# Attention scores and their gradients as 128-column products on four 32-row strips, in a kernel that computes a gated block and its gradients

## The chip, the cores and the metric

The kernel runs on one core of one Trainium2 chip, as one program. The metric is device time in microseconds (us), from the timed runs of the program; lower is better. The engines are named as in the profile: PE is TensorE (matrix products and transposes), ACT is ScalarE, DVE is VectorE, POOL is GpSimd, SP is the engine that issues most DMAs.

## What is computed

A forward pass of two branches mixed by a gate, and the gradients of all its inputs but one (everything in bf16, x is 2048 x 512):

```python
def _A_ref(x, wqkv, wo):                      # attention, 32 heads of 16, window 256
    q, k, v = split_heads(x @ wqkv)
    scores = einsum("bhqd,bhkd->bhqk", q, k) * (Dh ** -0.5)
    mask = (iq - ik >= 0) & (iq - ik < 256)
    p = softmax(where(mask, scores, -1e9))
    return merge_heads(einsum("bhqk,bhkd->bhqd", p, v)) @ wo

def _B_ref(x, W_gate, W_up, W_down):          # gated MLP, inner width 1376
    gate, up = x @ W_gate, x @ W_up
    return ((gate * (gate > 0)) * up) @ W_down

g = sigmoid((x * gate_w).sum(-1))
out = g * _A_ref(x, wqkv, wo) + (1 - g) * _B_ref(x, W_gate, W_up, W_down)
# outputs: out, and its gradients with respect to x, wqkv, wo, W_gate, W_up, W_down, gate_w
```

## The kernel before

It has three stages. The first (lines 189 to 456) computes the MLP branch, its weight gradients, and the inputs of attention's backward pass. The last (lines 920 to 997) sums the output and the gradient of x for 16 row tiles of 128. The change lies almost wholly in the stage between them, attention forward and backward (lines 458 to 916).

Attention works on four chunks of eight heads (`c`), and in each on 16 query blocks of 128 (`j`). A query block meets its own key block and the two before it. `project_parts` (lines 119 to 187) makes, for one chunk and four query blocks (a group), the tiles Q, dO, K and V with (head, dimension) on the 128 partitions, so that a strip of 32 partitions holds two heads of 16. K and V are kept in two copies, each with every second head's rows set to zero (`K0`, `K1`, lines 153 to 160).

A unit (lines 627 to 641) is one query block, one key block and one half of the chunk's heads, four heads: 90 units a chunk, 360 in all. `front` (line 643) computes its scores in one product of 128 rows and 512 columns (`ST`, line 649). The moving operand is a tile `z` in which the four strips of Q stand block-diagonally with zeros around them; `spread` (line 468) fills it with four DMAs a group. ACT takes the exponential (line 655), POOL masks the diagonal and the far key block with a 512-column `affine_select` (lines 657 and 660), and `front_dp` (line 663) makes the gradient with respect to the probabilities the same way (`dPT`, line 669). `gradp` (line 671) multiplies both on DVE. `rowsum` (line 676) makes 8 small products a unit into one PSUM bank, `BA`, from which POOL works out each query block's terms (`small_ops`, line 711). `flip` (line 694) transposes a unit's two results: 159 units by a DMA transpose that SP issues (line 697), 201 by eight transposes on TensorE into a PSUM bank of the tag `TR` (line 706) and one copy of 1024 columns, on ACT and DVE in turn. `cd_piece` (line 480) makes the products for the gradients of K and V from the flipped tiles. `grad_parts` (line 557) makes the weight gradients of the last chunk.

The order is written out by hand. The loop at line 821 goes through the units one by one. Each step issues the scores of unit n, DVE's product of unit n-1, the DMA flip of unit n-2, row sums and TensorE's flip of unit n-3, then `front_dp` of unit n, then CD pieces, and then, as a running credit allows (lines 872 to 897), one piece of the next group's projection or of the last chunk's weight gradients. PSUM has eight banks: four of the tag `M` (scores, their gradients, projections, weight gradients), two `TR`, one `CD`, one `BA`.

Of the kernel before, what the change touches and what calls it, by code (L numbers as in the profile page):

```python
# [22 lines left out]
def kernel(  # L23
# [82 lines left out]
    ZB = 2  # L106
    wq = ctx.enter_context(tc.tile_pool(name="wq", bufs=1))
    zt = [wq.tile([P, 2, TPG, NP, P], BF, tag=f"z{i}", name=f"z{i}") for i in range(ZB)]
# [4 lines left out]
    if True:  # L113
# [5 lines left out]
        def project_parts(c, tg):  # L119
# [3 lines left out]

            def mm(nm, which, eng):
                ps, tag, bufs, _ = pools["now"]
                pp = ps.tile([P, TGW], F32, tag=tag, bufs=bufs, name="pp")
                for cd in range(DC):
                    if which < 3:
                        nc.tensor.matmul(pp[:], lhsT=w_p[c][:, cd, which * P:(which + 1) * P], rhs=x_T[tg][:, cd, :],  # L129
                                         start=(cd == 0), stop=(cd == DC - 1))  # L130
                    else:
                        nc.tensor.matmul(pp[:], lhsT=w_p[c][:, cd, 3 * P:4 * P], rhs=da_T[tg][:, cd, :],
                                         start=(cd == 0), stop=(cd == DC - 1))
                if nm in ("Q", "dO"):
                    if nm == "Q":
                        t4["z"] = pjA.tile([P, 2, TGW], BF, tag="zT", name="zT")
# [8 lines left out]
                if nm in ("Q", "dO"):  # L145
                    if c == 0 and tg == 0:
                        w = ("Q", "dO").index(nm)
                        for k in range(NP):
                            rows = slice(32 * k, 32 * k + 32)
                            evac(zt[0][rows, w, :, k, :], dst[rows, :].rearrange("p (k q) -> p k q", k=TPG),  # L150
                                 (("dve", "act")[w] if k % 2 else "dve"))
                else:
# [9 lines left out]
            def tr(a_nm, b_nm):  # L162
                ps, tag, bufs, trt = pools["now"]
                pt = ps.tile([P, 2, TPG, P], BF, tag=trt, bufs=2, name="ptp")
# [11 lines left out]
            def tr_kv():  # L176
# [9 lines left out]
            return [lambda: mm("Q", 0, "dve"), lambda: mm("dO", 3, "dve"), tr_rows, lambda: mm("K", 1, "act"),  # L186
                    lambda: mm("V", 2, "act"), tr_kv]

    with ExitStack() as p1, tc.manual_schedule():
# [20 lines left out]
        def load_go(tg):  # L210
            flat = zt[tg // 2][:].rearrange("p w k h q -> p (w k h q)")
            go_in[tg] = flat[:, (tg % 2) * TPG * D:(tg % 2 + 1) * TPG * D].rearrange("p (t d) -> p t d", t=TPG)
            nc.sync.dma_start(go_in[tg], rows_of(go_d, tg))
# [186 lines left out]
        pools["now"] = (ps1, "tr", 2, "tr")  # L400
# [3 lines left out]
        for n in range(N1 + 8):  # L404
# [38 lines left out]
            if t in (NT + 3, NT + 5):  # L443
                i = (t - NT - 3) // 2
                nc.gpsimd.memset(zt[i][:, 0, :, :, :], 0.0)
                nc.vector.memset(zt[i][:, 1, :, :, :], 0.0)
            if n == N1 - 2:
                first = project_parts(*groups[0])
            for _ in range({N1 + 1: 2, N1 + 2: 0}.get(n, 1)):
                if first:  # L450
                    first.pop(0)()
# [7 lines left out]
    if True:  # L459
# [7 lines left out]
        pools["now"] = (ps, "M", 4, "TR")  # L467
        def spread(gi, k):
            rows = slice(32 * k, 32 * k + 32)
            nc.sync.dma_start(zt[gi % ZB][rows, :, :, k, :],  # L470
                              proj[groups[gi]]["z"][rows, :, :].rearrange("p w (k q) -> p w k q", k=TPG))

# [7 lines left out]
        def cd_piece(c, kb, qb, half, last):  # L480
# [4 lines left out]
            p2 = P2[(c, qb, kb, half)]  # L485
            for hh in range(HH):
                h = 2 * hh + half
                nc.tensor.matmul(cd[0][:, h, :], lhsT=p2[:, 0, hh, :], rhs=rq[:, h, 0:2 * Dh],  # L488
                                 start=cd[1], stop=True, skip_group_check=True)
                cd[1] = False  # L490
                nc.tensor.matmul(cd[0][:, h, 0:Dh], lhsT=p2[:, 1, hh, :], rhs=rq[:, h, 2 * Dh:3 * Dh],  # L491
                                 start=False, stop=True, skip_group_check=True)
# [47 lines left out]
        def load_wo():  # L540
            t = pjA.tile([P, 2, TGW], BF, tag="zT", name="wo_z")
# [15 lines left out]
        def grad_parts(c, rest=None):  # L557
# [13 lines left out]
            hold = {}  # L571

# [7 lines left out]
            def piece(part, t0, first, last):  # L580
                if first:
                    tag, bufs = ("TR", 2) if part == DC and rest is not None else ("M", 4)
                    hold[part] = ps.tile([P, 3, P] if part < DC else [P, D], F32, tag=tag, bufs=bufs, name="wps")
                wps = hold[part]
                for t in range(t0, t0 + 4):
                    go_, no_ = first and t == t0, last and t == t0 + 3
                    if part < DC:
                        nc.tensor.matmul(wps[:], lhsT=x_r[:, t, part * P:(part + 1) * P], rhs=sts[c][:, t, 0:3, :],  # L588
                                         start=go_, stop=no_)
                    else:  # L590
                        nc.tensor.matmul(wps[:], lhsT=sts[c][:, t, 3, :], rhs=rows[t], start=go_, stop=no_)
                if not last:
                    return None
                if part < DC:
                    ws = (gwp if rest is None else S2["t6"]).tile([P, 3, P], BF, tag="ws", bufs=2 if rest is None else 5, name="ws")
                    evac(ws[:], wps[:], "act" if rest is None or part % 2 else "dve")
                    return store(part, ws)
                if t0 + 4 < NT:
                    hold["half"] = gwp.tile([P, D], F32, tag="half", bufs=1, name="half")
                    evac(hold["half"][:], wps[:], "act")  # L600
                    for k in range(4, 8):
                        load_da(k)
                    return None
                ws = (gwp if rest is None else S2["t6"]).tile([P, D], BF, tag="ws", bufs=2 if rest is None else 5, name="ws")
                if "half" in hold:
                    nc.vector.tensor_tensor(out=ws[:], in0=hold["half"][:], in1=wps[:], op=ALU.add)
                else:
                    evac(ws[:], wps[:], "act")
                return store(part, ws)

            if rest is None:
                parts = [(DC, 0, NT // 2)] + [(p, 0, NT) for p in range(DC)] + [(DC, NT // 2, NT)]
# [6 lines left out]
            for part, a, b in parts:  # L619
                for t0 in range(a, b, 4):  # L620
                    out.append((lambda part=part, t0=t0, f=(t0 == a), l=(t0 + 4 == b): piece(part, t0, f, l), t0 + 4 < b))
# [5 lines left out]
        units = []  # L627
        for c in range(DC):
            for j in range(NT):
                kbs = [k for k in (j - 1, j, j - 2) if k >= 0]  # L630
                for half in range(2):
                    order = kbs if half or len(kbs) < 3 else [kbs[0], kbs[2], kbs[1]]
                    for ki, kb in enumerate(order):
                        u = Unit()
                        u.c, u.j, u.kb, u.half = c, j, kb, half
                        u.first = ki == 0 and half == 0
                        u.last = ki == len(kbs) - 1 and half == 1
                        u.role = ("d", "m", "f")[j - kb]
                        u.dma = (u.role == "d" or (u.role == "m" and half == 0 and j % 2 == 1)) and (c < DC - 1 or j < NT - 2)
                        units.append(u)  # L640
        NU = len(units)

        def front(u):
            tg, jl = u.j // TPG, u.j % TPG
            z = zt[(u.c * NTG + tg) % ZB]
            KTt = proj[(u.c, u.kb // TPG)][f"K{u.half}"]
            ksl = slice((u.kb % TPG) * P, (u.kb % TPG + 1) * P)
            ST = ps.tile([P, HH, P], F32, tag="M", bufs=4, name="ST")
            nc.tensor.matmul(ST[:], lhsT=KTt[:, ksl], rhs=z[:, 0, jl, :, :], start=True, stop=True)  # L649
            if u.dma or u.role == "d":  # L650
                u.PP = wk.tile([P, 2, HH, P], BF, tag="PP", bufs=5, name="PP")
                u.Pu, u.Pd = u.PP[:, 0, :, :], u.PP[:, 1, :, :]
            else:
                u.Pu = wk.tile([P, HH, P], BF, tag="Pu", bufs=3, name="Pu")
            nc.scalar.activation(u.Pu[:], ST[:], ACT.Exp)  # L655
            if u.role == "d":
                nc.gpsimd.affine_select(out=u.Pu[:], in_=u.Pu[:], compare_op=ALU.is_ge, fill=0.0, base=0,  # L657
                                        pattern=[[0, HH], [1, P]], channel_multiplier=-1)
            elif u.role == "f":
                nc.gpsimd.affine_select(out=u.Pu[:], in_=u.Pu[:], compare_op=ALU.is_ge, fill=0.0, base=-1,  # L660
                                        pattern=[[0, HH], [-1, P]], channel_multiplier=1)

        def front_dp(u):
# [364 lines left out]
```

## Time and profile before

| | us |
|---|---|
| timed runs: median of 3 (lowest, highest) | 968.82 (966.36, 969.21) |
| the profiled execution: its time | 971.04 |
| its span, first to last instruction | 969.0 |
| attention stage in it, first score product to the first product of the last weight gradients | 517.9 |

The profile page gives each engine's busy time and a map of 40 slices of the span. The trace behind it answers for a window, a line of the kernel, or a tile. Matrix products are pipelined, so one product's duration in the trace is its latency; what it costs TensorE is the distance from its start to the next start. A group's row in the profile reads: line, engine, operation, output and inputs with their shapes, count, then busy time in us and the mean duration of one in ns, then idle time before it and what ended it.

### The profile page before, as it was taken

The page shows a single profiled execution, that of the slowest core. Times are in us where ns is not written, and L with a number is a line of the kernel's source. Part 1 is how long each engine was busy: PE and PEld are TensorE (multiplying, and loading weights), DVE is VectorE, ACT ScalarE, POOL GpSimd, SP SyncE. Part 2 cuts the span into 40 slices and gives each one's busy share as a digit, 9 for nine tenths or more (in the row PEclk, how much of TensorE's full clock was granted, in tenths as well). Part 3 has the DMA queues.
Part 4 walks back from the last instruction along what each step waited for, and adds up shares of the span by engine and source line. Part 5 has one row for each costly group of instructions (what it writes and reads, how often), then busy time and mean ns, then how long its engine had stood idle before and what let it go on. Part 6 is the DMA issues. An engine that isn't in the chain of part 4 may idle for free.

```text
span 969.0 us, 27638 instructions
## 1 busy us (share of the span) xinstructions
PE 938.9 (97%) x11281; PEld 598.3 (62%) x11281; DVE 501.5 (52%) x918; ACT 473.8 (49%) x811; POOL 488.4 (50%) x936
## 2 busy tenths in 40 slices
PE   7999999999999999999999999989999999999998
PEld 4556555656567777676776677756777754444443
DVE  4443323323377777666776667765667613223322
ACT  5422322222378777667776667766677720001001
POOL 2644345444177667666676556665657622121211
PEclk9999999999999999999999999998999999999999
DMA  9988899996667598985889857899999969866760
GB/s 291 185 201 206 218 218 210 220 196 174 143 114 122 100 160 155 154 146 100 145 126 189 138 103 139 127 162 175 160 141 229 185 184 260 194 171 165 183 155 28
DMA packets 447415, 161.64 MB, mean 167 GB/s; under 512 B 365784, under 2 KB 444984, under 8 KB 447288
## 3 DMA queue, kind: packets, MB, share of 16 engines
q1 hardware_dynamic: 424888, 136.80, 73.8%
q10 hardware_dynamic: 20592, 17.84, 6.1%
q0 software_dynamic: 1808, 5.24, 1.5%
q8 instruction: 88, 1.44, 0.7%
q14 instruction: 39, 0.32, 0.1%
HBM read 38.44 MB, written 38.41 MB: 79 GB/s over the span
## 4 chain that ended last, share of the span: by engine, by line
PE 82%; DMA 6%; POOL 4%; SPq 2%; DVE 2%; ACT 1%; issue 1%; ACTq 0%; POOLq 0%; DVEq 0%
PE pt L706 9%; PE dxps L970 8%; PE ST L649 7%; PE dPT L669 7%; PE wps L373 6%; PE wps L588 4%; PE dxps L991 4%; PE BA L683 4%; PE pp L129 4%; PE bps L941 4%; PE CD L488 4%; PE dhps L326 3%; PE ups L326 3%; PE dps L375 3%; PE gps L326 3%; PE CD L491 2%
## 5 line engine op out<-in xcount | busy, mean ns | idle before, releaser
L674 DVE TENSOR_TENSOR Pd<-Pu,dPT 128x512 bf16<-128x512 bf16 x201 | 136.6, 681 | 64.9 <-POOL Pu L660 53.5
L655 ACT ACTIVATE Pu<-ST 128x512 bf16<-128x512 f32 x201 | 121.6, 606 | 58.9 <-PE ST L649 57.3
L649 PE MATMUL ST<-z,K 128*128 128x512 bf16 x360 | 136.8, 380 | 4.0 <-DVE Pd L674 1.7
L669 PE MATMUL dPT<-z,V 128*128 128x512 bf16 x360 | 137.2, 381 | 1.3 <-DVE Pd L674 1.1
L674 DVE TENSOR_TENSOR PP<-PP,dPT 128x512 bf16<-128x512 bf16 x159 | 108.4, 682 | 41.0 <-POOL PP L657 38.1
L657 POOL TENSOR_SCALAR_AFFINE_SELECT PP<-PP 128x512 bf16<-128x512 bf16 x128 | 81.3, 635 | 79.5 <-ACT PP L655 78.8
L655 ACT ACTIVATE PP<-ST 128x512 bf16<-128x512 f32 x159 | 95.7, 602 | 51.7 <-PE ST L649 42.0
L340 POOL TENSOR_TENSOR hT<-rg,upm 128x512 bf16<-128x512 bf16 x44 | 52.2, 1186 | 123.9 <-DVE upm L338 98.4
L488 PE MATMUL CD<-rq,p 128*128 128x32 bf16 x1440 | 109.7, 177 | 0.8 <-ACT rows_st L494 0.5
L373 PE MATMUL wps<-dgu_r,x_r 128*128 128x256 bf16 x704 | 105.6, 272 | 4.9 <-DVE wst L74 4.9
L491 PEld LDWEIGHTS <-p 128*128 128x128 bf16 x1440 | 86.4, 96 | 35.9 <-issue 3.1
L72 ACT COPY p<-pt 128x1024 bf16<-128x1024 bf16 x103 | 105.1, 1020 | 5.2 <-PE pt L706 2.5
L491 PE MATMUL CD<-rq,p 128*128 128x16 bf16 x1440 | 106.7, 169 | 0.0
L488 PEld LDWEIGHTS <-p 128*128 128x128 bf16 x1440 | 99.0, 96 | 1.7 <-issue 1.5
L660 POOL TENSOR_SCALAR_AFFINE_SELECT Pu<-Pu 128x512 bf16<-128x512 bf16 x112 | 71.0, 634 | 41.8 <-ACT Pu L655 40.1
L373 PEld LDWEIGHTS <-x_r 128*128 128x128 bf16 x704 | 68.8, 98 | 36.7 <-issue 6.3
L948 ACT COPY a_sb<-aps 128x512 f32<-128x512 f32 x16 | 9.4, 585 | 145.8 <-issue 133.1
L706 PE MATMUL pt<-ident,Pd 128*128 128x128 bf16 x804 | 78.4, 220 | 0.0
L706 PE MATMUL pt<-ident,Pu 128*128 128x128 bf16 x804 | 77.7, 219 | 0.0
L74 DVE COPY p<-pt 128x1024 bf16<-128x1024 bf16 x102 | 69.5, 681 | 6.1 <-PE pt L706 5.4
L332 ACT ACTIVATE rg<-gps 128x512 bf16<-128x512 f32 x44 | 26.3, 598 | 91.0 <-PE gps L326 49.6
L683 PE MATMUL BA<-KV,Pu 128*128 128x33 bf16 x804 | 66.6, 178 | 4.1 <-ACT BAs L689 4.0
(158 smaller groups left out, 1998.7 us busy)
## 6 DMA issues: line engine op xcount, KB each, us to landing
dqkvo_d<-rows_st SPq DMA_DIRECT2D x7, 1024.0 KB, 5.7
dar<-da_d SPq DMA_DIRECT2D x28, 256.0 KB, 4.3
hT_d<-hT ACTq DMA_DIRECT2D x44, 128.0 KB, 2.4
dgT_d<-dgu ACTq DMA_DIRECT2D x44, 128.0 KB, 2.8
duT_d<-dgu ACTq DMA_DIRECT2D x44, 128.0 KB, 2.8
duT_g<-duT_d SPq DMA_DIRECT2D x8, 640.0 KB, 5.2
dgT_g<-dgT_d SPq DMA_DIRECT2D x7, 640.0 KB, 9.1
gt<-hT_d SPq DMA_DIRECT2D x7, 640.0 KB, 5.7
```

The lines of the kernel that those rows point to most:

```text
L72: nc.scalar.copy(out, in_)
L326: nc.tensor.matmul(out[:], lhsT=w(c), rhs=x(c), start=(c == 0), stop=(c == DC - 1))
L373: nc.tensor.matmul(acc["w"][:, c, :], lhsT=x_r[:, t, c * P:(c + 1) * P], rhs=k.dgu_r[:, :, i, :], start=(go_ and c % 2 == 0), stop=no_, sk ...
L488: nc.tensor.matmul(cd[0][:, h, :], lhsT=p2[:, 0, hh, :], rhs=rq[:, h, 0:2 * Dh], start=cd[1], stop=True, skip_group_check=True)
L491: nc.tensor.matmul(cd[0][:, h, 0:Dh], lhsT=p2[:, 1, hh, :], rhs=rq[:, h, 2 * Dh:3 * Dh], start=False, stop=True, skip_group_check=True)
L649: nc.tensor.matmul(ST[:], lhsT=KTt[:, ksl], rhs=z[:, 0, jl, :, :], start=True, stop=True)
L655: nc.scalar.activation(u.Pu[:], ST[:], ACT.Exp)
L657: nc.gpsimd.affine_select(out=u.Pu[:], in_=u.Pu[:], compare_op=ALU.is_ge, fill=0.0, base=0, pattern=[[0, HH], [1, P]], channel_multiplier=-1)
L669: nc.tensor.matmul(u.dPT[:], lhsT=VTt[:, ksl], rhs=z[:, 1, jl, :, :], start=True, stop=True)
L674: nc.vector.tensor_tensor(out=u.Pd[:], in0=u.Pu[:], in1=u.dPT[:], op=ALU.mult)
L683: nc.tensor.matmul(BA[:, h, 0:33], lhsT=u.Pu[:, hh, :], rhs=kv[:, u.kb % TPG, h, 1:34], start=(u.first and hh == 0), stop=True, skip_group ...
L706: nc.tensor.transpose(pt[:, a, hh, :], src[:, hh, :], ident[:])
```

## The change

The zero-padded tile `z` and its DMAs are gone. A unit is now one strip of 32 partitions (two heads, `g` from 0 to 3) and two key blocks; a turn works on two units. The loop goes through 46 turns a chunk, 184 in all, for six turns per pair of query blocks: `d` and `e` units pair the diagonal and the far block, `m` units the two middle blocks. In each turn TensorE makes the scores of this turn's two units and the gradients of the last turn's two as 16 products of 32 rows and 128 columns, issued in rotation over the four strips. Each unit has a PSUM bank of its own: two banks `S`, two `D`. Projections, weight gradients and TensorE's flips share the two banks `tr`.

```diff
+                its = ((d, (0, 1)), (m, (2, 3)), (m, (0, 1)), (d, (2, 3)), (e, (0, 1)), (e, (2, 3)))
...
+                        u.dma = g % 2 == 0 and u.nb == 2 and (c > 0 or j > 0) and (c < DC - 1 or j < NT - 2)
...
+        def score(u, nm, w, out):
+            rows = slice(32 * u.g, 32 * u.g + 32)
+
+            def one(i, par):
+                qb, kb = u.blocks[i]
+                nc.tensor.matmul(out[:, i, par, :],
+                                 lhsT=proj[(u.c, kb // TPG)][f"{nm}{par}"][rows, (kb % TPG) * P:(kb % TPG + 1) * P],
+                                 rhs=proj[(u.c, qb // TPG)]["z"][rows, w, (qb % TPG) * P:(qb % TPG + 1) * P],
+                                 start=True, stop=True, skip_group_check=True)
+            return [lambda i=i, par=par: one(i, par) for i in range(u.nb) for par in range(2)]
+
+        def products(us, vs):
+            lists = []
+            for u in us:
+                u.S = ps.tile([P, 2, 2, P], F32, tag="S", bufs=2, name="S")
+                lists.append(score(u, "K", 0, u.S))
+            for v in vs:
+                v.D = ps.tile([P, 2, 2, P], F32, tag="D", bufs=2, name="D")
+                lists.append(score(v, "V", 1, v.D))
+            for r in range(4):
+                for fs in lists:
+                    if r < len(fs):
+                        fs[r]()
...
         def front(u):
-            ST = ps.tile([P, HH, P], F32, tag="M", bufs=4, name="ST")
-            nc.tensor.matmul(ST[:], lhsT=KTt[:, ksl], rhs=z[:, 0, jl, :, :], start=True, stop=True)
...
+            u.PP = wk.tile([P, 2, 4, P], BF, tag="PPm" if u.mid else "PP", bufs=4 if u.mid else 7, name="PP")
+            n = 2 * u.nb * P
+            nc.scalar.activation(u.PP[:, 0, 0:2 * u.nb, :].rearrange("p b q -> p (b q)"), flat(u.S[:], n), ACT.Exp)
+
+        def mask(u):
+            if u.mid:
+                return
+            same = all(qb == kb for qb, kb in u.blocks)
+            for b0, b1, up in ((0, 4, True),) if same else ((0, 2, True), (2, 4, False)):
+                out = u.PP[:, 0, b0:b1, :]
+                nc.gpsimd.affine_select(out=out, in_=out, compare_op=ALU.is_ge, fill=0.0, base=0 if up else -1,
+                                        pattern=[[0, b1 - b0], [1 if up else -1, P]], channel_multiplier=-1 if up else 1)
...
         def flip(u):
+            p2 = place(u)
             if u.dma:
...
+            pt = ps.tile([P, 2, 4, P], BF, tag="tr", bufs=2, name="pt")
+            n = 2 * u.nb
+            for a in range(2):
+                for b in range(n):
+                    nc.tensor.transpose(pt[:, a, b, :], u.PP[:, a, b, :], ident[:])
+            evac(p2[:, 0, 0:n, :], pt[:, 0, 0:n, :], "act")
+            evac(p2[:, 1, 0:n, :], pt[:, 1, 0:n, :], "dve")
```

A turn `k` of the new loop issues, in this order:

```diff
+                us = turns_[k] if k < NI else []
+                vs = turns_[k - 1] if 1 <= k <= NI else []
+                ws = turns_[k - 2] if 2 <= k < NI + 2 else []
...
+                for eng, f in now:
+                    if eng != "dma":
+                        f()
...
+                if us or vs:
+                    products(us, vs)
+                    cost += 0.44
+                for u in us:
                     front(u)
+                for u in us:
+                    mask(u)
+                for v in vs:
+                    gradp(v)
+                for v in vs:
+                    if v.dma:
+                        flip(v)
...
+                cost += some_sums(fresh)
+                for _ in range(4 if not us else 3):
+                    if cdq and closed.get(cdq[0][0:1] + cdq[0][2:3], k) + 3 <= k:
+                        cd_piece(*cdq.pop(0))
+                        cost += 0.2
+                for w in ws:
                     if not w.dma:
                         flip(w)
...
+                elif bg:
+                    left = max(1, until - k)
+                    credit += (BASE - cost if k > 3 else 0.0) + sum(b[0] for b in bg) / left
+                    while bg and (credit >= 0.5 * bg[0][0] or sum(b[0] for b in bg) > 2.2 * (until - k - 1)):
+                        credit -= bg[0][0]
+                        held = background()
+                    credit = max(-1.0, min(1.0, credit))
+                credit -= some_sums(True)
```

`some_sums` issues the row sums of blocks whose unit is at least two turns old, one query block after the other, since there is one bank `BA`. DVE's product (`gradp`), the small POOL operations and the CD products are as before but for their indices; the small operations come one to three turns after a query block's last row sum instead of three to seven steps. A projection is now nine pieces of two to eight products (before: five), a weight-gradient job eight pieces of two products (before: four of four); the partial sum that DVE added to finish one of them is gone. The DMA transposes number 168 (before 159). TensorE flips 184 units of eight transposes and 16 of four. In the first stage the 4 KB-per-partition buffers of `z` were also used for loads; four `wide` tiles of the same total size take their place, and the two memsets of `z` (line 445 on POOL, line 446 on DVE) are gone. At the end of the stage the early loads for the last stage are three, into three of these tiles, instead of two.

More of the change, by code (lines that the diff above doesn't have):

```diff
@@ L144, in mm @@
                 t4[nm] = dst
[L145 to L152, printed above, removed]
+                if nm in ("K", "V"):
                     for k in range(2):
@@ L466 @@
         ps = pps.enter_context(tc.tile_pool(name="attps", bufs=2, space=PSUM))
[L467 to L471, printed above, removed]
+        pools["now"] = (ps, "tr", 2)
         P2 = {}
@@ L625 @@
             pass
-        units = []
+        turns_ = []
         for c in range(DC):
[L629 to L633, printed above, removed]
-                        u = Unit()
[L635 to L640, printed above, removed]
@@ new lines, in gradp @@
+        def gradp(u):
+            n = 2 * u.nb * P
+            v = lambda a: u.PP[:, a, 0:2 * u.nb, :].rearrange("p b q -> p (b q)")
+            nc.vector.tensor_tensor(out=v(1), in0=v(0), in1=flat(u.D[:], n), op=ALU.mult)
+        sums = []
+        for k in range(0, NI):
+            c, j = turns_[k][0].c, turns_[k][0].j
+            if k and (turns_[k - 1][0].c, turns_[k - 1][0].j) == (c, j):
+                continue
+            its = [t for t in turns_ if t[0].c == c and t[0].j == j]
+            for qb in (j, j + 1):
+                part = [(u, i) for t in its for u in t for i in range(u.nb) if u.blocks[i][0] == qb]
+                for x, (u, i) in enumerate(part):
+                    sums.append((u, i, qb, x == 0, x == len(part) - 1))
@@ new lines, in rowsum @@
+        def rowsum(u, i, qb, first, last):
+            kb = u.blocks[i][1]
+            kv = proj[(u.c, kb // TPG)]["kv"]
+            if first:
+                BAt[(u.c, qb)] = ps.tile([P, HG, 50], F32, tag="BA", bufs=1, name="BA")
+            BA = BAt[(u.c, qb)]
+            for par in range(2):
+                h = 2 * u.g + par
+                nc.tensor.matmul(BA[:, h, 0:33], lhsT=u.PP[:, 0, 2 * i + par, :], rhs=kv[:, kb % TPG, h, 1:34],
+                                 start=(first and par == 0), stop=True, skip_group_check=True)
+                nc.tensor.matmul(BA[:, h, 33:50], lhsT=u.PP[:, 1, 2 * i + par, :], rhs=kv[:, kb % TPG, h, 0:17],
@@ L848 @@
[L848 to L855 removed]
+                                until -= 4
+                    if j == 6 and c > 0:
+                        ev.setdefault(k + 1, []).append(("dma", lambda c=c - 1: spill(c, NT // 2)))
```

367 lines of the change are left out of this document (169 added, 198 removed).

## The prediction

> **What bounds the kernel now.** I read the slices first, then busy time by stage, then TensorE's timeline, then the waits. The page, first its shares, then two rows of 40 slices:
>
> ```profile
> PE 938.9 (97%) x11281; PEld 598.3 (62%) x11281; DVE 501.5 (52%) x918; ACT 473.8 (49%) x811; POOL 488.4 (50%) x936
> ...
> PE   7999999999999999999999999989999999999998
> ...
> PEclk9999999999999999999999999998999999999999
> ```
>
> TensorE is full in every stage at the full granted clock. A modelled busy share is not proof, so the attention stage next: from the first score product (259.0) to the first product of the last weight gradients (776.9):
>
> ```profile
> core 0: us, PE busy (x) PEld busy (x) DVE busy (x) ACT busy (x) POOL busy (x), PEclk, DMA share, GB/s
> 259.00:776.90 517.90, 504.17 (x8625) 360.07 (x8626) 356.82 (x648) 370.04 (x632) 336.43 (x778) 0.99 0.84 147
> ```
>
> ScalarE, VectorE and GpSimd are 65 to 71% busy there, the DMA engines 84%. TensorE's timeline gives the price of each product from start to start:
>
> ```profile
> 500.78 0.38 PE L649 MATMUL ST<-z,K 128*128 128x512 bf16 x1
> 500.99 0.18 PE L683 MATMUL BA<-KV,PP 128*128 128x33 bf16 x1
> 501.02 0.17 PE L685 MATMUL BA<-KV,PP 128*128 128x17 bf16 x1
> ...
> 501.20 0.38 PE L669 MATMUL dPT<-z,V 128*128 128x512 bf16 x1
> 501.41 0.18 PE L488 MATMUL CD<-rq,p 128*128 128x32 bf16 x1
> ...
> 502.24 0.38 PE L706 MATMUL pt<-ident,Pu 128*128 128x128 bf16 x4
> 502.46 0.39 PE L706 MATMUL pt<-ident,Pd 128*128 128x128 bf16 x4
> 502.68 0.38 PE L669 MATMUL dPT<-z,V 128*128 128x512 bf16 x1
> 502.89 0.38 PE L649 MATMUL ST<-z,K 128*128 128x512 bf16 x1
> ```
>
> A 512-column product holds the engine 0.215 us (0.38 is its latency), eight small ones 0.205 (500.99 to 501.20), so 0.0256 each however narrow, and eight 128-column transposes 0.44, so 0.055 each. Four 384-column gradient products take 0.65 (the chain: eight in 1.30). The stage issues:
>
> - scores and gradients, 2 x 360 x 0.215 = 154.8
> - row sums and CD products, 5,760 x 0.0256 = 147.5
> - flips on TensorE, 201 x 0.44 = 88.4
> - 15 projections of 16 products and 8 transposes, 15 x 3.88 = 58.2
> - three chunks' weight gradients, 3 x (16 x 0.215 + 64 x 0.163) = 41.6
>
> Sum 490.5; the other 27.4 are waits and two short clock dips. TensorE's own work bounds the stage, so a product saved is time saved, until another engine is late.
>
> **The change, part by part.**
>
> *Scores and gradients.* Each 512-column product over four zero-padded strips becomes four 128-column products on 32 rows each: 2,880 of them, sixteen a turn, from four row groups in rotation. No run shown has a product on fewer than 128 rows. Ends: if only the engine's stream counts and four groups run fully side by side, 720 x 0.055 = 40; if they never overlap, 2,880 x 0.055 = 158; if they overlap but each start costs what a small product's start costs, 2,880 x 0.0256 = 74. I take 74: the small-product row already pays a weight load and a start for each product, which is what remains when the streams overlap. A turn's sixteen then cost 0.41 us where four products cost 0.86.
>
> The Trainium skill (TensorE: Matmul & The Clock Gate, Part 3, packing small matmuls) says that matmuls on different row groups run together, and gives 3.07x for four of 32 rows and 512 columns. By that, as an estimate, four of 0.215 take 0.28, so starts lie 0.022 apart and the term is 63 instead of 74. No run here shows it yet.
>
> *Going between forms.* Every turn goes from full-height products to strips and back, 370 times. The trace shows no such step. Low end 0: between transposes and products it shows no gap (502.46 to 502.68 to 502.89). High end 0.166: a 512-column product's latency 0.381 less its pace 0.215, as if nothing started before the last had ended. I take 0.04, near the row without a gap: 15 us; ends 0 and 61.
>
> *Flips.* 184 full and 16 half ones: 184 x 0.44 + 16 x 0.22 = 84.5 (88.4 before). Each copy is split, 512 columns to ScalarE and 512 to VectorE.
>
> *Row sums, CD, projections, gradients:* the same products in smaller pieces, 247.3 as before. New: projections and gradients share two banks ("tr") with the flips, where they had four ("M"). A gradient job holds one for eight pieces, so a flip then waits for the last one's copies; flips come once a turn, 2.5 us apart, and the copies take about 0.6, so I cost it nothing; without that cover 0.3 a turn in the 90 turns or so with gradients, 27 us.
>
> TensorE's sum: 84.5 + 247.3 + 74 + 15 = 421.
>
> *The other engines* (busy sums in the stage; rows):
>
> ```profile
> L657 POOL TENSOR_SCALAR_AFFINE_SELECT PP<-PP 128x512 bf16<-128x512 bf16 x128 | 81.3, 635 | 79.5 <-ACT PP L655 78.8
> ...
> masks.py:199 POOL TENSOR_SCALAR_AFFINE_SELECT ident<-ident 128x128 bf16<-128x128 bf16 x1 | 0.3, 292 | 0.1
> L250 POOL TENSOR_SCALAR_AFFINE_SELECT par<-par 128x4 f32<-128x4 f32 x1 | 0.2, 194 | 0.1
> ```
>
> GpSimd: 224 units now need two masks of 256 columns, 16 one of 512. Between 292 ns (128 columns) and 635 (512) a 256-column mask is 406: 448 x 0.406 + 16 x 0.635 = 192, against 240 x 0.635 = 152. So 336 + 40 = 376. ScalarE: 368 exponentials instead of 360, but 16 are half as wide; copies 184 x 0.585 + 16 x 0.376 = 114 against 104: 370 + 10 = 380. VectorE: 357 + about 9 = 366. All stay under 421, at 79 to 82% of the new stage.
>
> *DMA.* The 60 spreads of z go; transposes go from 159 to 168, still one issue of 1.27 us on SP per turn at most. P tiles go from 5 buffers to 7 + 4, so a late landing blocks exponentials later than now (two landings of 4.6 and 6.5 us stand in the chain at 638 and 648). The last chunk has a DMA share near 1.0, and squeezing it returns some of this; I count it in the waits.
>
> *Waits.* Now:
>
> ```profile
> DVE Pd L674 <- POOL Pu L660: 53.5, 66, 1.7
> ...
> PE BA L683 <- ACT BAs L689: 8.4, 9, 2.8
> ```
>
> VectorE waits for masks, but that seldom reaches TensorE today. In the new order a turn's gradient products need both D banks, so both VectorE products of the turn before. That loop is 0.41 issue + 0.18 latency + 2 x 0.68 = 1.95 us, under the mean turn of 421/184 = 2.29. It fits, with little slack where a mask is late. I raise the waits from 27 to 42 (bounds 20 and 80), since three engines go from some 69% to some 81%.
>
> Stage: 421 + 42 = 463, a saving of 55. In the first stage a 1.75 us memset of z on GpSimd lies on the chain at 150.95; it goes, worth 0 to 2, I take 1. The last stage issues the same products. Span 969.0 - 56 = 913; the profiled execution lies 2.0 above its span (971.0), and the median of the runs 2.2 below that: **913 us** for the timed runs.
>
> **Rivals.**
>
> 1. *Each change of form waits for the array to empty.* For: nothing here shows it free. Against: changes of kind cost nothing now. At 0.166 the term is 61, TensorE's sum 467, with waits of 33 a stage of 500: 950. The Trainium skill (TensorEngine Tiling (Array Packing), Key Properties) says that changing the tiling mode drains the engine; no trace here can show it, and this rival is what it would make.
> 2. *The row groups don't run side by side* (slower): each product then costs its stream, 0.055 as a transpose does, 158 in all, because the strips follow one another through the one engine. Sum 505, waits 27, stage 532: 982; with rival 1's price 1,029. It decides from 0.86 us a turn for products and changes of form, the price of today's four products. For: no row shows two products streaming at once.
> 3. *Masks.* Four of six turns need four masks (1.62 us), between the blocks' small GpSimd operations (eight per query block, 3.1 us). If each of those 123 turns ends one mask (0.41) late through the D banks, waits are 27 + 50, stage 498: 948. For: VectorE's longest waits are for GpSimd already.
> 4. *Lighter*: starts of strips cost less than a small product's, 40 in place of 74. Sum 387, and then the D-bank loop and ScalarE set the turn: waits of 48, stage 435: 885.
>
> **How the numbers follow.** Forecast 0.42 (890 to 935 by itself), lighter 0.11, masks 0.12, draining 0.12: faster 0.77. Draining and late masks together come out near the time of before: within 0.3%, about what a measurement of this kernel can tell from no change, 0.05. No overlap, slower: 0.18. The range, 878 to 980, leaves out the lower half of "lighter" and most of "no overlap", some 0.19.
>
> **What would show it.** The timeline of a turn: sixteen products starting 0.025 apart (0.055: rival 2); the gap at their ends (0.04, or 0.17: rival 1); masks of 256 columns near 406 ns; TensorE's waits for VectorE's products (rival 3) or for flips' copies; the stage's length 463. I am wrong if the stage stays above 500 with products 0.41 a turn and no gaps: then a bank or buffer, not TensorE, sets the turn.

## The result, and the profile after

The changed kernel takes **1010.25 us** (median of 4; 1006.18 to 1016.24) where the kernel before took 969.02 in the same job: a ratio of 1.0426, 95% interval 1.0359 to 1.0493. It is slower, and it lies outside the forecast range of 878 to 980. The profiled execution took 1011.85 us.

The page of the changed kernel, in the same rows as before:

```profile
span 1010.1 us, 32218 instructions
...
PE 895.1 (89%) x13219; PEld 585.2 (58%) x13337; DVE 499.7 (49%) x1013; ACT 467.0 (46%) x914; POOL 510.4 (51%) x1158
...
PE   8999999999888888888887888887888799999998
PEclk9999999999789898799997899997999799999999
```

TensorE is no longer full: its row falls to 8 and 7 in the 22 slices of the attention stage. The row below is the surprise. The granted clock was 9 nearly throughout before; now it dips in the same slices. By the trace's clock records the stage has 99.0 us at half clock, in 16 stretches of 3.4 to 13.7 us (before: 10.2 us in 2). It varies from one execution to the next: in the four timed runs the mean granted clock over the whole span was 0.963, 0.958, 0.948 and 0.941, and the times rose in that order, from 1006.18 to 1016.24 us.

The stage by itself, in the columns of the table by stage that was shown for before (busy time of each engine, granted clock, DMA share):

```profile
260.10:815.70 555.60, 458.80 (x10590) 344.09 (x10660) 359.31 (x750) 364.00 (x735) 361.01 (x1001) 0.91 0.80 135
```

The stage grew from 517.9 to 555.6, 37.7 of the 41 us; no engine is fuller than before, and the clock is 0.91 where it was 0.99. So something waits. One turn on TensorE, from its timeline:

```profile
519.58 0.61 PE L735 MATMUL pt<-ident,PP 128*128 128x128 bf16 x8
520.12 0.23 PE L641 MATMUL S<-zT,K 32*128 32x128 bf16 x2
520.12 0.23 PE L641 MATMUL D<-zT,V 32*128 32x128 bf16 x2
520.18 0.22 PE L641 MATMUL S<-zT,K 32*128 32x128 bf16 x2
520.19 0.22 PE L641 MATMUL D<-zT,V 32*128 32x128 bf16 x2
...
520.29 0.22 PE L641 MATMUL S<-zT,K 32*128 32x128 bf16 x2
520.30 0.22 PE L641 MATMUL D<-zT,V 32*128 32x128 bf16 x2
520.45 0.19 PE L702 MATMUL BA<-KV,PP 128*128 128x33 bf16 x1
```

The products themselves came out better than forecast. Four row groups start within some 10 ns of one another, the next four 0.055 later, and all sixteen within 0.18. The last group then streams 0.055 and the first full-height product follows 0.09 after that: 520.30 to 520.45 is 0.15. The eight transposes ahead take 0.54 to the next start where they took 0.44. So a turn pays 0.24 for products and 0.09 at each end.

What TensorE waited for, from the list of waits over the stage (us in total, times, longest), and the one wait of another engine that matters:

```profile
PE CD L483 <- ACT rows_st L489: 35.6, 55, 0.9
PE pp L134 <- DVE p L74: 16.3, 18, 1.9
PE pt L735 <- DVE p L74: 7.3, 8, 1.3
PE S L641 <- ACT PP L667: 7.3, 6, 3.3
PE D L641 <- DVE PP L681: 5.4, 17, 0.4
```

```profile
DVE p L74 <- ACT p L72: 146.4, 167, 3.7
```

None of the first three stood in the list of before: there the longest was BA's 8.4 us, and `CD` had next to nothing. Its row of before, whose last numbers are the idle time ahead of it:

```profile
L488 PE MATMUL CD<-rq,p 128*128 128x32 bf16 x1440 | 109.7, 177 | 0.8 <-ACT rows_st L494 0.5
```

In the new kernel a product for the gradients of K and V (`CD`) waits for ACT to copy the one CD bank out (`rows_st`, line 489), 55 times. Projections (`pp`) and flips (`pt`) wait for DVE's half of a flip's copy (line 74), and DVE's half had waited for ACT's half (line 72): 167 of 200 times. The two halves:

```profile
L72 ACT COPY p<-pt 128x512 bf16<-128x512 bf16 x184 | 108.4, 592 | 69.3 <-PE pt L735 67.6
L74 DVE COPY p<-pt 128x512 bf16<-128x512 bf16 x184 | 78.1, 425 | 134.0 <-ACT p L72 132.5
```

Splitting TensorE's stage by the distance from each start to the next gives this ledger, where a distance counts as the pace of its product, as a change of form, as loss to half clock, or else as a wait. "Own work" is products 44, changes of form 34, flips 85, row sums 73, CD 71, projections 58, weight gradients 41:

| us in the stage | before | forecast | after |
|---|---|---|---|
| TensorE's own work | 489 | 421 | 406 |
| lost to half clock | 3 | } 42 | 21 |
| waits | 26 | } | 129 |
| stage | 518 | 463 | 556 |

The 129 are: CD 45, products for their banks S and D 25, projections 21, flips 10, weight gradients 9, row sums 9, the rest 10.

### The profile page after: what moved, and what is told of

Read it like the earlier page. It is cut to its first block, busy times and chain, and to the rows that moved or that the text cites. A ratio compares the mean times of both kernels' runs of the same rounds, so it can differ in the third digit from the quotient of the medians.

```text
span 1010.1 us, 32218 instructions
## 1 busy us (share of the span) xinstructions
PE 895.1 (89%) x13219; PEld 585.2 (58%) x13337; DVE 499.7 (49%) x1013; ACT 467.0 (46%) x914; POOL 510.4 (51%) x1158
## 5 line engine op out<-in xcount | busy, mean ns | idle before, releaser
L681 DVE TENSOR_TENSOR PP<-PP,D 128x512 bf16<-128x512 bf16 (+1 forms) x368 | 230.9, 668 | 32.6 <-PE D L641 21.9
L667 ACT ACTIVATE PP<-S 128x512 bf16<-128x512 f32 (+1 forms) x368 | 197.3, 587 | 94.8 <-PE D L641 71.3
L675 POOL TENSOR_SCALAR_AFFINE_SELECT PP<-PP 128x256 bf16<-128x256 bf16 (+1 forms) x464 | 176.8, 417 | 125.4 <-ACT PP L667 125.0
L72 ACT COPY p<-pt 128x512 bf16<-128x512 bf16 (+1 forms) x200 | 114.4, 576 | 77.0 <-PE pt L735 75.2
L735 PE MATMUL pt<-ident,PP 128*128 128x128 bf16 x1536 | 128.4, 232 | 7.7 <-DVE p L74 7.3
L702 PE MATMUL BA<-KV,PP 128*128 128x33 bf16 x1440 | 103.8, 181 | 2.9 <-ACT BAs L708 2.3
L735 PEld LDWEIGHTS <-PP 128*128 128x128 bf16 x1536 | 97.6, 103 | 9.0 <-issue 8.8
L704 PE MATMUL BA<-KV,PP 128*128 128x17 bf16 x1440 | 99.4, 171 | 0.0
L702 PEld LDWEIGHTS <-PP 128*128 128x128 bf16 x1440 | 83.8, 97 | 23.1 <-issue 4.4
L641 PE MATMUL S<-zT,K 32*128 32x128 bf16 x1440 | 83.7, 229 | 10.7 <-ACT PP L667 7.3
L641 PE MATMUL D<-zT,V 32*128 32x128 bf16 x1440 | 83.4, 228 | 5.8 <-DVE PP L681 5.4
L704 PEld LDWEIGHTS <-PP 128*128 128x128 bf16 x1440 | 84.2, 97 | 5.9 <-issue 4.2
```

The source lines that it names most:

```text
L72: nc.scalar.copy(out, in_)
L641: nc.tensor.matmul(out[:, i, par, :], lhsT=proj[(u.c, kb // TPG)][f"{nm}{par}"][rows, (kb % TPG) * P:(kb % TPG + 1) * P], rhs=proj[(u.c, q ...
L667: nc.scalar.activation(u.PP[:, 0, 0:2 * u.nb, :].rearrange("p b q -> p (b q)"), flat(u.S[:], n), ACT.Exp)
L675: nc.gpsimd.affine_select(out=out, in_=out, compare_op=ALU.is_ge, fill=0.0, base=0 if up else -1, pattern=[[0, b1 - b0], [1 if up else -1, ...
L681: nc.vector.tensor_tensor(out=v(1), in0=v(0), in1=flat(u.D[:], n), op=ALU.mult)
L702: nc.tensor.matmul(BA[:, h, 0:33], lhsT=u.PP[:, 0, 2 * i + par, :], rhs=kv[:, kb % TPG, h, 1:34], start=(first and par == 0), stop=True, s ...
```

## The experiments

The theory at this point: the new order of issue costs the time, by two banks. (a) A turn issues up to three CD pieces in a row. When a piece ends a key block, ACT must copy the bank before the next piece starts, and that copy stands behind the turn's two exponentials on ACT. The old loop (line 873) took a second piece when that one ended a key block, so that the border fell between steps; the new one takes pieces without regard to it. (b) Each flip's copy is in two halves that read one PSUM bank, and they run one after the other. Rivals: the strips themselves (changes of form, or products that gain little), and the clock.

| run | us | ratio to before, 95% | stage | at half clock |
|---|---|---|---|---|
| before | 969 | 1 | 517.9 | 10 |
| after | 1010.25 | 1.0426 (1.0359 to 1.0493) | 555.6 | 99 |
| e1_cd | 977.67 | 1.0043 (0.9991 to 1.0095) | 521.5 | 72 |
| e2_copy | 1002.97 | 1.0337 (1.0299 to 1.0375) | 547.6 | 89 |
| e3_cd_copy | 960.13 | 0.9880 (0.9842 to 0.9918) | 500.3 | 24 |
| e4_full | 1042.81 | 1.0739 (1.0696 to 1.0782) | 589.1 | 10 |
| e6_full_e3 | 1000.12 | 1.0314 (1.0279 to 1.0349) | 543.5 | 0 |
| e5_serial | 1011.71 | 1.0433 (1.0408 to 1.0459) | 557.8 | 89 |
| e9_one_strip | 1229.07 | 1.2677 (1.2550 to 1.2804) | 777.9 | 495 |
| e10_split | 987.74 | 1.0188 (1.0109 to 1.0267) | 533.3 | 55 |
| e7_one | 958.64 | 0.9884 (0.9863 to 0.9904) | 496.9 | 38 |
| e8_bg | 962.48 | 0.9922 (0.9896 to 0.9947) | 505.8 | 38 |

The times are medians. Stage and half clock come from one profiled execution of each kernel; those of e3 and e7 took 954.74 and 951.36 us, 5 and 7 under their medians, the others lie within 3.5 us of theirs. The runs were timed in three further jobs, in which the kernel before took 971.29 (e1 to e4), 969.70 (e5 to e8) and 968.98 us (e9, e10), so differences of a few us between jobs mean little.

### The CD bank alone (e1_cd)

When a key block ends within the next two pieces, the pieces up to that border go ahead of the turn's products, so that ACT's copy has the rest of the turn:

```diff
+                ahead = 0
+                if any(piece[-1] for piece in cdq[:2]):
+                    while cdq and closed.get(cdq[0][0:1] + cdq[0][2:3], k) + 3 <= k:
+                        piece = cdq.pop(0)
+                        cd_piece(*piece)
+                        cost += 0.2
+                        ahead += 1
+                        if piece[-1]:
+                            break
...
-                for _ in range(4 if not us else 3):
+                for _ in range((4 if not us else 3) - ahead):
```

> The changed kernel, but in turns where the CD pieces cross from one key block to the next, the pieces up to the border are issued ahead of the turn's products, so that ScalarE's copy of the one CD bank runs before its two exponentials and not behind them. Theory (single banks that TensorE waits for: CD 45 us, tr 50 us, the S and D loop 25 us): the 45 us of TensorE's waits at CD products fall below 10, and the time falls by 25 to 45 us, to 965 to 985 us. Rival (the turn is set by the chain exponential, mask, VectorE product, D bank, and TensorE only waits elsewhere for it): the waits at CD move to the S and D products, and the time stays within 10 us of 1010. Second rival (the halved clock, 99 us of the stage, makes TensorE late): waits fall little, the time stays.

977.67 us, 33 less than the changed kernel (37 by the ratios); the stage is 521.5. Its waits and its stage:

```profile
PE CD L483 <- ACT rows_st L489: 1.4, 3, 0.5
```

```profile
259.90:781.40 521.50, 455.79 (x10659) 345.16 (x10660) 360.71 (x750) 364.18 (x736) 361.26 (x1002) 0.93 0.86 143
```

55 waits for the copy became 3, and by the ledger all waits at CD fell from 45 to 10. The work of every engine is the same, so this is the wait's price, with the little that the clock gained by it (72 us at half against 99): most of the loss hung on one bank.

### Whole copies (e2_copy), and both (e3_cd_copy)

```diff
+        copier = {"i": 0}
...
-            evac(p2[:, 0, 0:n, :], pt[:, 0, 0:n, :], "act")
-            evac(p2[:, 1, 0:n, :], pt[:, 1, 0:n, :], "dve")
+            copier["i"] += 1
+            evac(p2[:, :, 0:n, :], pt[:, :, 0:n, :], ("act", "dve")[copier["i"] % 2])
```

> The changed kernel, but each TensorE flip is copied out of its bank by one engine, ScalarE and VectorE in turn, as before the change, and not half by each. Theory (the two halves read one bank and run one after the other: VectorE waits 146 us in 167 places for ScalarE's half, and the tr bank comes free late): VectorE's wait for ScalarE's copy disappears, TensorE's waits at projections, weight gradients and flips (about 50 us) halve, and the time falls by 15 to 35 us, to 975 to 995 us. Rival (VectorE has time to wait, and a 1024-column copy holds the bank as long as two halves in a row): the time stays within 8 us of 1010.

> Both of the last two edits. Theory (independent bank waits on TensorE): the savings add, 935 to 965 us, and with TensorE busier the stretches at half clock shrink from 99 us to under 50. Rival (one loop over the D banks sets the turn): no more than the better of the two alone.

Whole copies alone: 1002.97, a gain of 7 us where 15 to 35 were expected, and hardly clear of the spread: the intervals of the two ratios overlap. DVE's wait for ACT's half is gone, projections' waits fall from 21 to 15, but the CD waits stay and take up the rest:

```profile
PE CD L483 <- ACT rows_st L489: 38.2, 54, 1.3
```

Both: 960.13, 1.2% under the kernel before, a small gain whose interval is clear of 1. The parts don't add, 33 + 7 against 50: the second is worth 7 while CD stands in the way and 18 once it doesn't. The stage of both:

```profile
258.30:758.60 500.30, 442.55 (x10659) 337.25 (x10660) 346.33 (x652) 351.55 (x636) 361.01 (x1002) 0.98 0.87 148
```

Clock too is back at 0.98. By the ledger its waits are 88 and its clock loss 7; own work is the same 406.

### The strips undone (e4_full, e6_full_e3)

The same order of work, each product over all 128 rows at once; e4 on the changed kernel, e6 on e3:

```diff
-            rows = slice(32 * u.g, 32 * u.g + 32)
+            rows = slice(0, P)
```

> The changed kernel with the strips undone: every score and gradient product reads all 128 rows instead of its strip's 32, with the same 128 columns, banks and order; the scores then sum four strips, so this leaves the separation of heads out. No change of form is left and no two products can run side by side: 16 products should cost 0.89 us a turn instead of about 0.22, and the two gaps of 0.09 go. Theory (TensorE's own order and its waits set the stage): 184 x 0.48 = 88 us more work, partly in place of waits: 1050 to 1095 us, and the half clock stays in part, as it comes from waits. Rival (the clock is halved because strips count as little activity): the half clock nearly disappears, under 20 us of the stage, and 20 us come back: 1030 to 1075.

> The kernel with both edits (CD border pieces ahead, whole copies), and on top every score and gradient product on all 128 rows, as in the earlier run of the same form; the separation of heads is left out. It tells what the strips are worth once the bank waits are reduced. Theory (TensorE's order sets the stage): 16 products cost 0.89 us a turn, the two gaps of 0.09 go: 184 x 0.48 = 88 us more against 960, less some waits: 1015 to 1040. Rival (waits on other engines set the turn, so the strips' saving is not seen): under 990.

A turn's products in e4, from its timeline, and the stages of e4 and e6:

```profile
518.75 0.38 PE L134 MATMUL pp<-x,p 128*128 128x512 bf16 x1
518.96 0.28 PE L641 MATMUL S<-zT,K 128*128 128x128 bf16 x2
519.07 0.28 PE L641 MATMUL D<-zT,V 128*128 128x128 bf16 x2
...
519.74 0.28 PE L641 MATMUL D<-zT,V 128*128 128x128 bf16 x2
519.86 0.18 PE L702 MATMUL BA<-KV,PP 128*128 128x33 bf16 x1
```

```profile
258.40:847.50 589.10, 515.31 (x10659) 451.90 (x10660) 364.25 (x750) 365.40 (x736) 360.56 (x1001) 0.99 0.72 127
```

```profile
258.40:801.90 543.50, 507.49 (x10658) 446.21 (x10659) 346.84 (x651) 355.98 (x637) 360.56 (x1002) 1.00 0.79 136
```

Now the sixteen lie 0.055 apart, 0.90 in all, with no gap at either end: the change of form is a matter of strips. The times are under what the theories expected: 1042.81 fits the rival alone, as does the half clock of 10 us, and 1000.12 lies between the two ranges given for e6. And this takes the change apart. The new order with full-height products costs 71 us in the stage (517.9 to 589.1): 46 by the two banks (589.1 to 543.5) and 26 that remain. The strips then **gain** 33 (589.1 to 555.6), or 43 where the two banks are out of the way (543.5 to 500.3; 40 by the medians). TensorE's own work fell by 83 either way; the other half went into more waits (34, in e6 to e3) and half clock (7). That TensorE comes sooner to the same banks would explain the waits; no run shows it by itself.

### Issue order (e5_serial)

All four products of a unit, then all four of the next, in place of the rotation:

```diff
-            for r in range(4):
-                for fs in lists:
-                    if r < len(fs):
-                        fs[r]()
+            for fs in lists:
+                for f in fs:
+                    f()
```

> The changed kernel with the same 16 strip products a turn, but issued unit by unit, the four of one strip after one another, in place of the rotation over four strips. It tells what the half clock follows. Theory (products in one strip follow one another at 0.055, so a turn's sixteen take about 0.7 us instead of 0.22, and TensorE is busy for as long as with full-height products): if the clock follows the time in which TensorE streams anything, the half clock falls from 99 us to under 40, and the time rises by less than the 85 us of added products, to 1030 to 1060. Rival (a product on 32 rows counts little, however long it streams): the half clock stays at 70 us or more, and the time rises to 1060 to 1100. If the rotation buys nothing, both stay at 1010.

It was meant to take the overlap away, and it did not: 1011.71. A turn in its timeline, where the program puts eight score products ahead of the first gradient product:

```profile
521.52 0.24 PE L641 MATMUL S<-zT,K 32*128 32x128 bf16 x2
521.54 0.24 PE L641 MATMUL D<-zT,V 32*128 32x128 bf16 x2
521.58 0.23 PE L641 MATMUL S<-zT,K 32*128 32x128 bf16 x2
```

Two scores start, then two gradients 0.02 later, then the next scores: gradient products started while six score products ahead of them in the program had not, their row groups being busy. So the order of issue within sixteen doesn't matter here, and the run says nothing of what the overlap is worth. The Trainium skill (TensorE: Matmul & The Clock Gate, Part 3) states that matmuls start and end strictly in program order; by the starts in this trace they don't, and the measurement decides. Its distance of about 4 ns between starts of different tiles agrees with the 3 ns of the changed kernel.

### One row group only (e9_one_strip)

Every product reads the first strip, on the changed kernel:

```diff
-            rows = slice(32 * u.g, 32 * u.g + 32)
+            rows = slice(0, 32)
```

> The changed kernel with all 16 products of a turn read from the first strip of 32 rows, so that they can only follow one another: the other strips' heads are left out. It tells whether the half clock follows how long TensorE streams or how many rows it streams on. If time: the products take 0.89 us a turn, as with all 128 rows, and the half clock falls from 99 us to about the 10 us seen there, with a time near that run's 1043 plus 33 us for the changes of form: 1060 to 1085. If rows: the half clock stays above 60 us or grows, and with it the time: 1080 to 1120.

This does take the overlap away:

```profile
258.40:1036.30 777.90, 725.48 (x10661) 570.49 (x10662) 368.65 (x750) 375.17 (x737) 361.73 (x1002) 0.68 0.53 98
```

The products lie 0.055 apart at full clock, as in e4, but the stage is 189 us longer than e4's and 495 us of it run at half clock (e4: 10). At 1229.07 us the run is far above both ranges that were given, on the side of "rows". Both have the same products in the same order at the same pace; they differ in the rows that stream, 32 against 128, in the changes of form, and in what follows from those. The changes of form alone don't do it: e3 has as many, with 24 us at half clock. Nor was TensorE idler: in a stretch at full clock right before a long one at half, its records cover 95% (9.64 of 10.10 us), and e4 kept its clock with 87%:

```profile
302.70:312.80 10.10, 9.64 (x205) 8.12 (x205) 6.93 (x13) 6.34 (x13) 5.33 (x16) 1.00 0.48 78
```

So TensorE's being busy isn't by itself what keeps its clock: full-height streams did, and thin ones did not. The Trainium skill (TensorE: Matmul & The Clock Gate, Part 1) says that the clock is released by TensorE's activity over windows of some 3.4 us; the shortest half-clock stretches here, 3.4 us, agree. The changed kernel stands between: sixteen thin products and a wait in most turns.

### More changes of form (e10_split)

On e3, in 150 turns a full-height row-sum piece goes between the score and the gradient products, which makes 300 more changes of form:

```diff
-                    products(us, vs)
+                    products(us, [])
+                    if sums and sums[0][0].at + 2 <= k and not sums[0][3] and not sums[0][4]:
+                        rowsum(*sums.pop(0))
+                        cost += 0.1
+                    products([], vs)
```

> The kernel with both edits, and in 150 of the 184 turns one row-sum piece of full height, moved up from its place a little later, stands between the score products and the gradient products: 670 changes of form in place of 370, with the same products. Theory (each change costs TensorE 0.09 us, which nothing hides): 300 x 0.093 = 28 us more, 980 to 995. Rival (the gaps lie beside waits for banks, so that more of them cost little): 960 to 972.

987.74, 28 us more than e3, and 300 changes at 0.093 are 28. But the agreement is luck, because the edit does more than it was meant to. A turn's scores lie on two strips and its gradients on the other two, so the split takes away their overlap as well:

```profile
540.46 0.40 PE L641 MATMUL S<-zT,K 32*128 32x128 bf16 x8
540.78 0.19 PE L702 MATMUL BA<-KV,PP 128*128 128x33 bf16 x1
...
540.98 0.40 PE L641 MATMUL D<-zT,V 32*128 32x128 bf16 x8
541.30 0.19 PE L702 MATMUL BA<-KV,PP 128*128 128x33 bf16 x1
```

Eight products on two strips take 0.32 to the next product, 0.23 without the change of form: as long as sixteen on four. In 150 turns that is some 34 us more, so TensorE's own work grew by about 62, the stage by 33 (500.3 to 533.3), and its clock fell a little as well (55 us at half, against 24). About half of the added work must have gone where TensorE had waited. So the run doesn't show what a change of form costs the kernel; the gap of 0.09 itself is seen at the changes in the traces, and e4's trace, which has no change of form, has no such gap.

### What is left: the shared banks (e7_one, e8_bg)

e7 opens at most one new background job per turn that needs a `tr` bank; e8 issues the background ahead of the flips. Both on e3:

```diff
+                    opened = 0
...
+                        opened += not held
+                        if opened > 1 and bg[0][0] > 0.0 and sum(b[0] for b in bg) <= 1.6 * (until - k - 1):
+                            break
```

```diff
                 for w in ws:
                     if not w.dma:
-                        flip(w)
                         cost += 0.444 if w.nb == 2 else 0.222
...
+                for w in ws:
+                    if not w.dma:
+                        flip(w)
```

(in e8 the last three lines stand behind the background).

> The kernel with both edits, and a turn opens at most one new background job that takes a tr bank, where it could open two. Theory (TensorE waits some 22 us for tr banks at projections, above all when a second product group starts in the turn in which the first one ended): those waits fall to about 10 us, the time to 945 to 955. Rival (they are moved to the next turn, or the pieces pile up before a group's end): 957 to 970.

> The kernel with both edits, and each turn's background pieces ahead of its flips. Theory (a projection then finds the bank of the last turn's flip free, whose copy had half a turn more): waits at projections fall by 10 us, those at flips rise by less: 948 to 958. Rival (the flips now wait for the projections' copies, behind VectorE's two products): 958 to 970.

e7 gives 958.64, e3's time within the spread of both, though projections' waits fell from 15 to 9; the longest wait is now weight gradients' for a DMA:

```profile
PE wps L588 <- DMA dar<-da_d: 8.5, 5, 3.8
```

e8 gives 962.48: projections' waits fall below 1, but flips wait 25 and CD 25 in their place. The waits on these banks move rather than go, and both times lie in the ranges of the rivals.

## Why the prediction was wrong

- **Waits, 42 with bounds of 20 and 80: the step that failed.** They were 129, and 21 more of clock, 150 in all and 108 over the term; less the 15 by which TensorE's own work was lighter than forecast, that is the 93 by which the stage missed its 463. I reckoned with masks, both D banks and late DMAs, and never with the one CD bank, because it cost nothing before. But that was the doing of the old order: the loop that is replaced held the rule that put a key block's end between steps, and the diff shows the new one without it (`range(4 if not us else 3)`). e1 undoes it for 33 us.
- **The shared `tr` banks, "I cost it nothing".** The cover I named was a copy of 0.6 us. The two halves take 0.59 on ACT and then 0.43 on DVE, and ACT's stands behind the exponentials. The price I gave for the cover gone, 27 us, is near the 21 of projections and 10 of flips, but by luck: I had flips wait for the copies of gradient jobs, and mostly it was projections that waited for the flips' copies. Whole copies bring 7 to 18 back (e2, e3).
- **The clock, taken as full.** It cost 21 us on TensorE, some 0.21 for each us at half clock. The four timed runs agree: by their clocks and spans the slowest had about 120 us at half clock and the fastest 74, and it took 10 us longer, an estimate of 0.22. Nothing in the trace of before shows thin products, so it couldn't be read there, but it belonged among the bounds.
- **Changes of form, 0.04 each:** mis-sized. They took 0.09 to 0.10 (0.08 from a row sum into strips), the term is 34 and not 15, inside the bounds of 0 and 61. Rival 1's mechanism is there at 0.56 of its price: the Trainium skill (TensorEngine Tiling (Array Packing), Key Properties) says that a change of tiling mode drains the engine, and the gaps agree, 0.09 at each end, none in e4.
- **Products, 74:** too dear. Starts of different strips are 3 ns apart, so sixteen take 0.24 and not 0.41, 44 in all, near rival 4's 40. This and the last point cancel: products and changes together took 0.42 a turn (0.24 + 2 x 0.09) where the two terms make 0.49 (0.41 + 2 x 0.04), and own work of 406 against 421 was right within 4%.
- **Rival 2**, which held the chance of slower, is refuted by the starts; the time ended on its side for another reason.
- **Rival 3**, masks: no. DVE's products wait for a mask 1.6 us in all. The price of a mask was right, 409 ns against an estimate of 406, and the busy sums of ACT, DVE and POOL were close, 364, 359 and 361 against 380, 366 and 376:

```profile
L675 POOL TENSOR_SCALAR_AFFINE_SELECT PP<-PP 128x256 bf16<-128x256 bf16 x448 | 167.0, 409 | 110.2 <-ACT PP L667 109.8
```

- The prediction's last sentence named the outcome: a stage above 500 without dear products means that a bank or buffer sets the turn. Its signs held only in part, with products at 0.24 a turn and gaps of 0.09, and it was given no chance of its own. A rival "the new order meets a bank with one buffer", priced at the copy's 0.38 plus ACT's two exponentials at 0.60 for each of the 64 key blocks, would have been up to some 100 us (45 were measured), and would have moved the forecast to no change or slower.

Open: the 26 us by which the new order with full-height products is behind the old one even without the two banks' waits (e6 against before), and how the 88 us of waits in e3 divide among causes; e7 and e8 only moved them. Strips in the old order of work were not tried. What exactly the clock follows is inferred from e3, e4, e6 and e9, not measured by itself. What a change of form costs on the path, beyond its gap, is open too.

## What to carry to other kernels

When a change replaces a hand-written order, list each buffer that exists once and ask which line of the old order kept it from being waited for; price it as the copy plus what is queued ahead of the copy on its engine. Work that shrinks on the fullest engine is worth only what the banks behind it allow: here 83 us less work gave 33 or 43. Products on row strips do overlap and pay, but keep them together in the program, since each way in and out leaves TensorE a gap of 0.09 us, and products on two strips alone overlap only two deep.

## What the runs showed that I had not expected

- A stream of thin products did not hold the clock: 495 us at half clock with all products on one strip, 10 with the same products on 128 rows. TensorE was not idler with the thin ones: its records cover 95% of a stretch right before the clock fell, against 87% of the stage with full height.
- Products on an idle row group started ahead of earlier ones whose row group was busy (e5), so rotating them by hand brought nothing (1010.25 against 1011.71 us).
- Going from full-height products to strips or back leaves a gap of 0.08 to 0.10 us each time, whether 512-column products, transposes or small products stand on the other side.
